# How the opening's shared query rows are loaded: 32 rows in place of 31, and ahead of the query tiles

## The chip, the cores and the metric

The kernel runs on one core of a Trainium2 chip. A core has a matrix engine (TensorE, PE in the profile), a vector engine (VectorE, DVE), a scalar engine for activations (ScalarE, ACT), a general engine (GpSimd, POOL) and SyncE (SP), which here does nothing but issue transfers. Each engine takes its instructions in order and waits for others by semaphores. Transfers between the chip's memory (HBM) and the on-chip memory (SBUF, 128 partitions) are made by 16 DMA engines that all issuing engines share. The metric is the device time of one execution in microseconds, taken as the median of several runs.

## The reference

The inputs are q, k and v of shape (8, 8, 576, 64): 8 batches, 8 heads, 576 rows, 64 columns. An attention without a score matrix is followed by a Fourier mixing block with a feed-forward layer:

```
q_s = softmax(q) over the 64 columns of a head
k_s = softmax(k) over the 576 rows
kv  = k_s^T v                      per batch and head, 64 x 64
x   = q_s kv                       laid out as (8, 576, 512)
u   = x + real(fft(fft(x, rows), columns))
out = u + relu(layernorm(u) @ w_ch1) @ w_ch2      w_ch1 512 x 2048, w_ch2 2048 x 512
```

All is float32.

## The kernel before

The eight batches are worked through one after another: while TensorE multiplies the feed-forward layers of one batch, the attention and the Fourier block of the next are prepared. The first batch has nothing to hide behind, so it has an opening of its own. Every step of the program carries a time as a number; the steps are sorted by it and each engine executes its share in exactly that order (a schedule written by hand, the text `OPENING`). The numbers set the order only: nothing waits for a clock, everything waits for data.

The opening loads, all issued by SyncE in the order that the list `order` in `loads_first` gives, unless it is said otherwise:

- four key tiles `ks` (L305), 128 partitions of 576 numbers, 288 KB each
- two query tiles `own` (L314), 128 partitions of two rows of 512 numbers, 512 KB each; tiles A and B of the script come from the first, C and D from the second
- the shared rows `tail`: the Fourier block folds row s with row 576 - s, and what does not fit in the tiles of 128 is collected from two batches in one tile, 4 groups of 32 partitions. The first partition of each group is a special row (row 0 or row 288 of a batch), the other 31 are consecutive rows. The function `shared` loads the 31 rows of each group (L295, four transfers), `shared_firsts` the four first rows (L298, issued by ScalarE as its first instruction)
- the values `v` in two column halves; each half is a transfer of 512 rows (L309) and one of the last 64 rows (L310)
- three tables of cosines and sines (L342 to L346), then eleven pieces of the feed-forward weights, called words (L369, 512 KB each), and behind these the keys and values of batch 1 (L676, L688) and more words (L371)

The weights come as 64-bit words and are converted on the chip (`convert`: ScalarE L396 and L397, VectorE L390 and L393, GpSimd L398); later words take the place of converted ones, so their loads are issued as conversions finish.

The computation of the opening, in the order of TensorE: transposes of the keys' exponentials (L561, L569), transposes of query tiles A and B (L984), products of keys and values for heads 0 to 3 (L585), transposes of C (L984), products for heads 4 to 7 (L585), transposes of D, then query times kv for the tiles (L839) and the transposes of the shared tile t. VectorE takes the maxima of the key tiles (L553) and of A, B, C, D and t in this order (L967); GpSimd subtracts them for A, B and C, VectorE for D and t (L972); ScalarE takes the exponentials (L976). VectorE scales the product (L588) once all of L585 is done. The matrix engine is also given a few products without a use (`warm`, L269).

For later batches the shared rows are loaded by `t_rows`: four transfers of 32 rows issued by SyncE (L337), and the four first rows later, on SyncE too (L338).

Of the kernel before, what the change touches and what calls it, by code (L numbers as in the profile page):

```python
# [46 lines left out]
P = 128  # L47
B, H, S, DH = 8, 8, 576, 64
# [10 lines left out]
Q = 32  # L59
# [79 lines left out]
class _Block:  # L139
# [134 lines left out]
    def loads_first(self, fetch):  # L274

        nc, b = self.nc, 0
        at = 2 * NF * D

        def place(n):
            nonlocal at  # L280
            at += n
            return self.big[:, at - n:at]

        own = [place(2 * D).rearrange("p (c n) -> p c n", n=D) for _ in range(2)]
        tail = place(D)
        at = 3 * NF * D - 5 * P - NC * D - NR * S
        ks, v = [place(S) for _ in range(NR)], place(NC * D).rearrange("p (c n) -> p c n", n=D)
        self.at_start = ks, v, own, tail
        load = nc.sync.dma_start

        def shared():
            flat = self.q[b:b + 2].rearrange("b s n -> (b s) n")
            for i in range(4):
                a = i * S // 2 + P
                load(tail[i * Q + 1:(i + 1) * Q], flat[a + 1:a + Q])  # L295

        def shared_firsts():
            nc.scalar.dma_start(tail[0:P:Q], self.q[b:b + 2].rearrange("b s n -> (b s) n")[::S // 2])  # L298

        def table():  # L300
            t = self.small.tile([P, 1], F32, tag="root", name="root", bufs=1)
            nc.scalar.activation(t[:], self.eps[:], ACT.Exp)

        def keys(r):
            load(ks[r], self.kT[b, r * P:(r + 1) * P, :])  # L305

        def values(r):
            cols = slice(r * P, (r + 2) * P)
            load(v[:, 0:4, cols], self.v[b, 0:512, cols].rearrange("(c p) n -> p c n", p=P))  # L309
            load(v[64:, 4, cols], self.v[b, 512:, cols])  # L310

        def queries(i):
            fours = self.q[b].rearrange("(a p) n -> p a n", a=2)
            load(own[i], fours[(1, S // 2 - P)[i]:(1, S // 2 - P)[i] + P])  # L314

        each = lambda f: [lambda r=r: f(r) for r in range(NR)]
        order = [shared_firsts, lambda: nc.gpsimd.memset(v[0:64, 4, :], 0.0), table, *each(keys), lambda: queries(0), lambda: queries(1),
                 shared, lambda: values(0), lambda: values(2), self.tables, *(lambda i=i: fetch(i) for i in range(11))]
        later = [step for _, step in self.keys_to(1) + [(0, self.prepare)] + self.values_to(1, 0)]
        return [(i / 100, step) for i, step in enumerate(order)] + [(18 + i / 100, step) for i, step in enumerate(later)]  # L320

# [147 lines left out]
    def load(self, n):  # L469

        if n >= len(self.plan):
            return
        k = (n + 3) % 4
        w = self.big[:, k * NP * HD:(k + 1) * NP * HD]
        self.nc.sync.dma_start(w[:, :self.plan[n].shape[1]], self.plan[n])
        self.stream[n] = w.rearrange("p (a n) -> p a n", n=HD)
# [1516 lines left out]
```

## Time and profile before

| | us |
|---|---|
| median of 3 runs | 1017.97 |
| lowest and highest run | 1017.58, 1018.14 |
| the profiled execution | 1019.2 |
| its span, first to last instruction | 1017.4 |
| busy: PE, DVE, ACT, POOL | 994.0, 718.5, 495.3, 442.1 |

All times of the trace are microseconds from the start of the span. "SPq" is SyncE's queue, whose only instructions are the issues of transfers; the duration of one is the time that the issue held the queue, not that of the transfer. PEld is the loading of weights into TensorE. The granted clock is the share of full speed at which TensorE was allowed to run. The idle time in square brackets at the end of a row is how long the engine stood before it, and what ended that. Where an engine waits for several things, the profile names the one that came last by its reckoning.

### The profile page before, as it was taken

The numbers are of one execution on the slowest core, as the hardware profiler recorded it, in microseconds if no ns is written. First come the engines' busy times: TensorE is split into PE (matmuls) and PEld (weight loads), VectorE is DVE, ScalarE is ACT, GpSimd is POOL, SyncE is SP. The second block draws the span as 40 slices with busy tenths as digits, with TensorE's granted clock in tenths as the row PEclk, the third lists the DMA queues.
The fourth block names the chain that finished last, engine by engine and source line by source line (L and its number), as shares of the span: only waits on it lengthen the run. The fifth ranks groups of instructions, "written<-read, shape, count | busy, mean of one in ns | idle before, by whom it ended". The sixth has DMA issues, their size and how long they took to land.

```text
span 1017.4 us, 19783 instructions
## 1 busy us (share of the span) xinstructions
PE 994.0 (98%) x7546; PEld 853.8 (84%) x7546; DVE 718.5 (71%) x1355; ACT 495.3 (49%) x1285; POOL 442.1 (43%) x445
## 2 busy tenths in 40 slices
PE   5899999999999899999999999999999999999998
PEld 4764454788888799889988998899888998998897
DVE  4888898657675687678756886678656935685563
ACT  4576633682368327751776257724782242151200
POOL 3354430258445547465656556564646360040000
PEclk7999999999999999999999999999999999999999
DMA  7977499686999757776769577947654755675573
GB/s 229 264 259 257 158 244 328 228 234 217 322 328 241 243 198 263 222 223 225 270 213 253 195 258 246 259 175 262 230 187 167 263 194 198 225 268 183 181 253 131
DMA packets 123495, 236.36 MB, mean 232 GB/s; under 512 B 24124, under 2 KB 88380, under 8 KB 112776
## 3 DMA queue, kind: packets, MB, share of 16 engines
q1 hardware_dynamic: 123024, 234.56, 70.8%
q8 instruction: 60, 0.98, 0.4%
q14 instruction: 35, 0.29, 0.1%
q10 hardware_dynamic: 296, 0.27, 0.1%
q0 software_dynamic: 80, 0.26, 0.1%
HBM read 199.93 MB, written 39.06 MB: 235 GB/s over the span
## 4 chain that ended last, share of the span: by engine, by line
PE 85%; DVE 7%; DMA 4%; issue 1%; SPq 1%; POOL 1%; ACT 1%; DVEq 0%; POOLq 0%
PE bb L1543 15%; PE ba L1543 10%; PE bc L1543 10%; PE bb L1670 10%; PE ba L1670 7%; PE bc L1670 7%; PE bb L1640 5%; PE bc L1478 2%; PE two L839 2%; DMA big<-w1s 2%; PE one L754 2%; PE two L1206 1%; PE two L1263 1%; PE bb L1759 1%; PE ba L1478 1%; PE ba L1759 1%
## 5 line engine op out<-in xcount | busy, mean ns | idle before, releaser
L1543 PE MATMUL bb<-unT,big 128*128 128x256 f32 x768 | 183.2, 380 | 0.2 <-DVE u L1513 0.2
L1543 PEld LDWEIGHTS bb<-unT,big 128*128 128x128 f32 x768 | 144.8, 190 | 21.0 <-DVE u L1513 1.0
L1555 ACT ACTIVATE big<-big 128x512 f32<-128x512 f32 x96 | 59.8, 629 | 147.7 <-DVE big L1554 141.1
L1543 PE MATMUL ba<-unT,big 128*128 128x256 f32 x512 | 124.1, 382 | 2.8 <-DMA big<-w1s 2.7
L1543 PE MATMUL bc<-unT,big 128*128 128x256 f32 x512 | 121.5, 380 | 0.1
L816 ACT ACTIVATE qT<-q 32x128 f32<-32x128 f32 x384 | 117.9, 307 | 5.9 <-DVE q L806 0.7
L1543 PEld LDWEIGHTS ba<-unT,big 128*128 128x128 f32 x512 | 95.4, 190 | 17.0 <-DMA big<-w1s 3.2
L1543 PEld LDWEIGHTS bc<-unT,big 128*128 128x128 f32 x512 | 96.9, 190 | 13.7 <-DVE big L1554 0.5
L1513 DVE TENSOR_TENSOR u<-bb,s 128x512 f32<-128x512 f32 x66 | 45.2, 685 | 88.3 <-PE bb L1543 70.6
L1670 PE MATMUL bb<-big 128*128 128x128 f32 x848 | 103.8, 276 | 0.2 <-DVE u L1677 0.2
L1670 PEld LDWEIGHTS bb<-big 128*128 128x128 f32 x848 | 98.9, 192 | 1.0 <-DVE u L1677 1.0
L1389 POOL COPY unT<-unT 32x256 f32<-32x256 f32 x98 | 42.0, 428 | 91.4 <-DVE unT L1381 87.2
L1620 POOL TENSOR_TENSOR x<-x,big 128x512 f32<-128x512 f32 x45 | 61.0, 1368 | 46.0 <-DVE big L1677 19.7
L1616 DVE TENSOR_TENSOR big<-big 128x512 f32<-128x512 f32 x98 | 79.9, 843 | 0.0
L1670 PE MATMUL ba<-big 128*128 128x128 f32 x640 | 79.0, 276 | 0.0
L1670 PEld LDWEIGHTS ba<-big 128*128 128x128 f32 x640 | 75.0, 192 | 0.8
L1389 ACT COPY unT<-unT 32x256 f32<-32x256 f32 x126 | 50.7, 402 | 32.1 <-DVE unT L1381 30.3
L803 POOL TENSOR_TENSOR q<-q,qm 128x512 f32<-128x512 f32 x24 | 25.8, 1073 | 91.1 <-DVE qm L798 55.7
L404 POOL TENSOR_TENSOR big<-big 128x512 f32<-128x512 f32 x24 | 30.4, 1268 | 68.8 <-ACT big L1555 68.8
L1640 PE MATMUL bb<-big 128*128 128x256 f32 x256 | 58.3, 379 | 0.0
L1554 DVE TENSOR_TENSOR big<-bc,u 128x512 f32<-128x512 f32 x64 | 44.0, 688 | 16.5 <-PE bc L1543 15.7
L1640 PEld LDWEIGHTS bb<-big 128*128 128x128 f32 x256 | 48.0, 190 | 6.1
(335 smaller groups left out, 1914.5 us busy)
## 6 DMA issues: line engine op xcount, KB each, us to landing
big<-w2d SPq DMA_DIRECT2D x67, 1024.0 KB
big<-w1s SPq DMA_DIRECT2D x64, 896.0 KB
big<-w2s SPq DMA_DIRECT2D x16, 1024.0 KB
big<-in_w_dram SPq DMA_DIRECT2D x21, 512.0 KB
w2d<-big SPq DMA_DIRECT2D x42, 256.0 KB
kb<-in_kT_dram SPq DMA_DIRECT2D x28, 320.0 KB
q<-in_q_dram SPq DMA_DIRECT2D x28, 256.0 KB
vt<-in_v_dram SPq DMA_DIRECT2D x84, 80.0 KB
```

The source lines that it names most:

```text
L404: e1.tensor_tensor(out=to(4), in0=at(2), in1=at(3), op=ALU.add)
L816: nc.scalar.activation(to[t, i * Q:i * Q + Q], one, ACT.Exp)
L1389: copy(to, of)
L1478: nc.tensor.matmul(po[:], lhsT=h[:, f, i * P:(i + 1) * P], rhs=self.w2sb[:, f, :], start=(f == 0), stop=(f == NF - 1))
L1513: plus = lambda t: V.tensor_tensor(out=temp(t), in0=box["bb"][:], in1=box["s1"][:], op=ALU.add)
L1543: nc.tensor.matmul(bank()[:, i, :], lhsT=w[:, WA_AT[m], k * P:(k + 1) * P], rhs=self.unT[g][:, B_AT[m], k, :], start=first and i == 0 and ...
L1554: steps = [(0, lambda: V.tensor_tensor(out=hp(i), in0=bank()[:], in1=u()[:], op=ALU.add)), (0.8, lambda: nc.scalar.activation(hp(i), hp(i) ...
L1555: (0.8, lambda: nc.scalar.activation(hp(i), hp(i), ACT.Relu))]
L1616: e.tensor_tensor(out=to(o), in0=to(x), in1=to(y), op=op)
L1620: E.tensor_tensor(out=x, in0=x, in1=tile(m), op=ALU.add)
L1640: nc.tensor.matmul(box[name][:, i, :], lhsT=h[p][:, A_AT[m], i * P:(i + 1) * P], rhs=self.stream[n][:, p, :], start=p == 0 and (m != 1 or ...
L1670: nc.tensor.matmul(box[place[n]][:, i, :], lhsT=own(m)(A_AT[n])[:, f, :], rhs=w[:, r // 2, r % 2 * P:r % 2 * P + P], start=first and f == ...
```

## The change

Each of the four transfers of shared rows takes 32 rows in place of 31, beginning with partition 0 of its group, so that it writes the group's first partition as well, with a row that does not belong there. The step moves from behind the two query tiles to ahead of them. The step that loads the four special rows, now issued by SyncE in place of ScalarE, moves from the start of the list to where the shared rows stood, behind the query tiles, and writes the right rows over the wrong ones. The transfers of keys, queries, values, tables and words keep their sizes and their order among themselves.

```
         def shared():
...
-                load(tail[i * Q + 1:(i + 1) * Q], flat[a + 1:a + Q])
+                load(tail[i * Q:(i + 1) * Q], flat[a:a + Q])

         def shared_firsts():
-            nc.scalar.dma_start(tail[0:P:Q], self.q[b:b + 2].rearrange("b s n -> (b s) n")[::S // 2])
+            load(tail[0:P:Q], self.q[b:b + 2].rearrange("b s n -> (b s) n")[::S // 2])
...
-        order = [shared_firsts, lambda: nc.gpsimd.memset(v[0:64, 4, :], 0.0), table, *each(keys), lambda: queries(0), lambda: queries(1),
-                 shared, lambda: values(0), lambda: values(2), self.tables, *(lambda i=i: fetch(i) for i in range(11))]
+        order = [lambda: nc.gpsimd.memset(v[0:64, 4, :], 0.0), table, *each(keys), shared, lambda: queries(0), lambda: queries(1),
+                 shared_firsts, lambda: values(0), lambda: values(2), self.tables, *(lambda i=i: fetch(i) for i in range(11))]
```

## The prediction

> **What bounds the kernel now.** I read the page first for the whole (the chain that ended last is 85% TensorE), then the same chain cut to the first 60 us, because only the opening's loads are touched. Columns: start us, duration us, what the chain stood on.
>
> ```profile
> PE 85%; DVE 7%; DMA 4%; issue 1%; SPq 1%; POOL 1%; ACT 1%; DVEq 0%; POOLq 0%
> ```
> ```profile
> 4.83 3.75 SPq L295
> ...
> 8.63 12.45 DMA big<-in_v_dram
> ...
> 21.13 2.40 PE two L585 x40
> 23.53 1.05 PE tr L984 x4
> 24.58 1.98 PE two L585 x40
> 26.55 0.58 PE tr L984 x4
> 27.14 0.64 PE two L839 x32
> ...
> 58.56 3.75 DMA big<-in_w_dram
> ```
>
> From 4.83 to 21.13 us the chain is SyncE issuing the fourth shared transfer (L295) and then the first value load (L309 and L310), which needs 12.45 us. Only then do the products of keys and values (L585) start. The time line of SyncE's queue and the stretches say why (start, duration; then per stretch: length, busy us of PE, PEld, DVE, ACT, POOL, granted clock, DMA share, GB/s):
>
> ```profile
> 3.61 4.97 SPq L295 DMA_DIRECT2D big<-in_q_dram  x4
> 8.63 2.41 SPq L309 DMA_DIRECT2D big<-in_v_dram  x1
> 11.08 2.46 SPq L310 DMA_DIRECT2D big<-in_v_dram  x1
> 13.59 0.58 SPq L309 DMA_DIRECT2D big<-in_v_dram  x1
> 14.21 2.32 SPq L310 DMA_DIRECT2D big<-in_v_dram  x1
> 20.06 10.19 SPq L369 DMA_DIRECT2D big<-in_w_dram  x8
> ```
> ```profile
> 10.00:11.50 1.50, 0.13 (x2) 0.00 (x0) 1.41 (x3) 0.96 (x2) 1.50 (x2) 1.00 0.07 26
> 16.00:20.00 4.00, 0.00 (x0) 0.00 (x0) 0.00 (x0) 0.00 (x0) 0.00 (x0) 0.50 0.84 269
> 55.00:60.00 5.00, 5.00 (x25) 4.41 (x24) 4.86 (x8) 5.00 (x10) 2.71 (x3) 1.00 0.16 56
> ```
> ```profile
> DMA packets 19, 0.04 MB, mean 26 GB/s; under 512 B 0, under 2 KB 0, under 8 KB 19
> ```
>
> Between 10.0 and 11.5 us the only traffic is 19 packets (the last line is for that stretch), one per 79 ns, and the mean share of the 16 DMA engines is 0.07, which is one engine of sixteen. So the four shared transfers of 31 rows, 124 packets of one 2 KB row, run on a single engine: 124 x 79 ns = 9.8 us. SyncE's issues stall behind them (2.41, 2.46 and 2.32 us where the same kind costs 0.58), every later transfer has a part queued on that engine, and between 16 and 20 us all compute engines stand still.
>
> By the Trainium skill, "DMA: Bandwidth & Descriptors", section "Why a DMA increments its semaphore by 16 and not by 1", a transfer issued from SyncE is spread over the largest number of engines up to 16 that divides its outer dimensions: 31 rows get one engine, 32 rows sixteen. The trace agrees on the 31 rows (share 0.07).
>
> **The change, part by part.**
>
> (a) *32 rows instead of 31.* Do 32 rows spread? The kernel has such transfers later (L337, four of 32 rows, and L338, which waits for their landing):
>
> ```profile
> 549.86 2.14 SPq L337 DMA_DIRECT2D q<-in_q_dram  x4
> 557.98 0.58 SPq L338 DMA_DIRECT2D q<-in_q_dram  x1
> ```
>
> 128 packets of 79 ns on one engine are 10.1 us; these had landed 8.1 us after the first issue, in a full queue. So they ran on more than one. I take full spreading. The pace comes from VectorE's waits, where the fourth key tile lands at 7.29 and the first query tile at 8.70:
>
> ```profile
> 3.60 1.53 DVE L553 TENSOR_REDUCE km<-big 128x1 f32<-128x576 f32 x2 [2.45 <-DMA big<-in_kT_dram]
> 7.29 0.75 DVE L553 TENSOR_REDUCE km<-big 128x1 f32<-128x576 f32 x1 [0.60 <-DMA big<-in_kT_dram]
> 8.70 1.28 DVE L967 TENSOR_REDUCE qm<-big 128x8 f32<-128x512 f32 x2 [0.65 <-DMA big<-in_q_dram]
> 11.51 1.28 DVE L967 TENSOR_REDUCE qm<-big 128x8 f32<-128x512 f32 x2
> 20.27 0.69 DVE L967 TENSOR_REDUCE qm<-big 128x8 f32<-128x512 f32 x1 [7.48 <-DMA ft<-in_ft_dram]
> 20.87 1.28 DVE L972 TENSOR_TENSOR big<-big,qm 128x512 f32<-128x512 f32 x2
> ```
>
> 512 KB in 1.41 us. The shared rows are 256 KB, so 0.70 us in place of 9.8 us.
>
> (b) *Ahead of the queries.* Keys keep their place. Shared rows land at 7.29 + 0.70 = 8.0, queries at 8.70 + 0.70 = 9.4 and 10.8. That delays the first query tile's chain (maximum, subtract, exponential, transpose) by 0.70 us. Before, it was hidden behind the wait for values; now it counts.
>
> (c) *First rows behind them on SyncE.* The issue leaves ScalarE's queue, where nothing waited for it: nothing gained. On SyncE it writes into rows that the four transfers write, so it has to wait until these land. The same pattern later does wait:
>
> ```profile
> SPq L338 <- DMA q<-in_q_dram: 11.0, 3, 5.4
> ```
>
> Behind the waiting instruction stand the values, tables and words. Wait until 8.0 to 8.2, issue 0.6 (L338 above 0.58), so values are issued from about 8.8, against 8.63 before: no loss. Their data queue behind the queries anyway: 10.8 + 1.41 (512 KB) + 0.18 (64 KB) = 12.4 for the first pair, 14.0 for the second. Bounds: 12.4 by the stream, 13.1 if the first one takes from its issue at 8.8 as long as the first key tile (issued at 0.74, seen at 3.60: 2.86 us for 288 KB) plus 0.8 for the larger size and 0.6 for a late issue. I take 12.4 to 13.1.
>
> (d) *What is late next.* TensorE takes its work in the written order: transposes of A and B, then the products.
>
> ```profile
> 11.58 1.71 PE L984 MATMUL tr<-ident,big 128*128 128x128 f32 x8 [1.45 <-ACT big L976]
> 26.27 0.28 PE L585 MATMUL two<-big 128*64 128x64 f32 x4
> 25.41 0.43 PE L585 MATMUL two<-big 128*64 128x64 f32 x4
> ```
> ```profile
> 9.18:12.59 3.41, 1.79 (x11) 1.19 (x11) 3.31 (x7) 2.17 (x5) 2.36 (x3) 0.96 0.28 88
> 12.59:16.00 3.41, 0.70 (x4) 0.30 (x2) 0.19 (x1) 1.40 (x3) 1.38 (x5) 0.50 0.65 197
> 19.42:22.83 3.41, 1.70 (x32) 1.71 (x34) 1.89 (x3) 1.23 (x2) 0.00 (x0) 0.50 0.90 296
> 22.83:26.24 3.41, 3.41 (x54) 2.96 (x52) 1.06 (x3) 0.58 (x1) 0.00 (x0) 0.54 0.95 295
> 26.24:29.66 3.42, 3.42 (x144) 2.93 (x142) 2.59 (x8) 1.28 (x3) 0.53 (x2) 1.00 1.02 310
> ```
>
> A's transposes move from 11.58 to 12.28. The granted clock falls to 0.50 near 12.6, and as 9.2 to 12.6 gets no busier I keep that. Four transposes cost 0.58 at full and 1.05 at half clock (chain above): A ends about 13.3, B 14.35. Values are there by 13.1, so the products start at 14.35, not 21.13: 6.8 us earlier.
>
> The clock then decides the rest. Before, a stretch of 3.41 us that was half busy (1.70) was followed by 0.50, one wholly busy (3.41) by 1.00. Now 12.6 to 16.0 is wholly busy, so I take full clock from 16.0. Four products cost 0.28 against 0.43, a factor 0.65. First forty: 14.35 + 1.65 at half, the rest 0.75 x 0.65 = 0.5, end 16.5. C's transposes 0.6, 17.1. Second forty 2.40 x 0.65 = 1.56, 18.65. D's transposes 0.58: the product at 27.14 starts at about 19.25. Shift: 27.14 - 19.25 = **7.9 us**.
>
> The window of about 3.41 us after which sustained work lifts the clock is what the Trainium skill states ("TensorE: Matmul & The Clock Gate", "Part 1: The HAM clock gate"); the trace agrees in that both clock changes lie on borders of such stretches.
>
> VectorE and ScalarE are no bound; the rows of before:
>
> ```profile
> 21.58 1.23 ACT L976 ACTIVATE big<-big 128x512 f32<-128x512 f32 x2 [7.09 <-DVE big L972]
> 22.85 0.69 DVE L945 TENSOR_REDUCE qrec<-big 128x8 f32<-128x512 f32 x1 [0.70 <-ACT big L976]
> 33.23 1.71 PE L1216 MATMUL two<-ft,eo 128*128 128x144 f32 x12
> ```
>
> Maxima of C and D end at 12.8 + 0.7 = 13.5, the shared maximum (0.69) at 14.2, the two subtractions at 15.45, ScalarE's two exponentials (1.23) by 16.1, the sums (0.69 and two small steps) by 17.3, and the normalizing is wanted only after 18.65. The shared rows have long landed, so the wait until 20.27 goes.
>
> (e) *After the opening.* All order is by dependence, so the shift should carry on if the DMA stream keeps up: the three tables, 1043 KB by their shapes, end at 14.0 + 2.9 = 17 (first used at 33.23 before, so at 25.3 now), eleven words of 1.41 us at 32.5. The next load on the chain, the word at 58.56, is issued when a conversion frees its place, and in 55 to 60 us the DMA engines are at share 0.16, so there is room. The rest of the chain, 85% of it TensorE, holds no work tied to a time of its own.
>
> **Sum.** The profiled execution has a span of 1017.4 and took 1019.2 us; 1019.2 - 7.9 = 1011.3. It stands 1.2 above the median of the runs, 1017.97, so against that: 1017.97 - 7.9 = **1010.1 us**.
>
> **Rivals.**
>
> *The clock stays at half* until 19.4: first forty end 16.75, C 17.8, second forty 19.9, D 20.5; gain 6.65, time 1011.3. Until 26.2: D ends at 21.25 and the next 2.4 us of TensorE (L839 and transposes) take 1.3 more; gain 4.6, time 1013.4. For it: the clock kept 0.50 for 13.6 us before. Against: two of those four stretches were idle or nearly so.
>
> *The DMA stream does not follow*, since first word, next keys and values queue as before. Then the fetch at 58.56 is late instead. Before it SyncE issued this:
>
> ```profile
> 49.38 3.90 SPq L371 DMA_DIRECT2D big<-in_w_dram  x3
> ```
>
> That ends at 53.28, 5.3 us before 58.56. Were it not to move at all, the gain is 5.3: 1012.7 us. Against: the issues at 8.63 to 20.06 lose their stalls.
>
> *Slower: 32 rows still on one engine, ahead of the queries.* 128 packets of 79 ns from 7.29 end at 17.4; the first query tile lands at 8.70 + 10.1 = 18.8, B's transposes end at 14.35 + 9.4 = 23.8, the products start 2.6 us later than before: 1020.6. It decides from a shared transfer longer than about 7.5 us. Against: the 8.1 us above.
>
> *No change*: the values wait on something else than that engine, and 21.13 stays. Against: share 0.07 at 10 to 11.5.
>
> **How the numbers follow.** Forecast 0.62, its own range 1009.0 to 1011.0; clock late 0.19; stream behind 0.11; slower 0.04; no change 0.03; 0.01 for a gain over 9 us (no drop to half clock at 12.6). Forecast, late clock and part of the stream's case give 1008.6 to 1013.2. A change of 0.2% (2.0 us) is about what can be told from none. Faster: 0.62 + 0.19 + 0.11 + 0.01 = 0.93.
>
> **What would show it.** Shared transfers issued at about 0.4 us each without a stall near 4 us; a wait of SyncE before the first rows ending near 8; DMA above 250 GB/s from 10 to 12; VectorE's first query maximum near 9.4; L585 starting near 14.3; clock 1.00 from 16; L839 near 19.3; the word's fetch near 50.7. I am wrong if L585 starts after 16, or if the shift at 60 us is smaller than at 20.

## The result and the profile after

The changed kernel took 1008.68 us (median of 4 runs, 1007.74 to 1011.98), the kernel before 1017.78 us beside it. The ratio is 0.9925 with a 95% interval of 0.991 to 0.9941: 7.6 us faster, between 6.0 and 9.2. (Amounts in us that stand beside a ratio are worked out from it. The two medians alone lie 9.1 us apart.) Two later series of the same kernel gave 0.9922 (0.9909 to 0.9935) and 0.9933 (0.9919 to 0.9946). The forecast was 7.9 us.

The profiled execution took 1011.98 us with a span of 1010.2, so it lies at the upper end of its runs, as the profiled one of before did. Its span is 7.2 us shorter. SyncE's queue and the chain of the opening after the change (start, duration):

```profile
0.74 1.82 SPq L305 DMA_DIRECT2D big<-in_kT_dram  x4
2.60 1.82 SPq L295 DMA_DIRECT2D big<-in_q_dram  x4
4.47 0.94 SPq L314 DMA_DIRECT2D big<-in_q_dram  x2
8.76 0.69 SPq L298 DMA_DIRECT2D big<-in_q_dram  x1
9.50 0.39 SPq L309 DMA_DIRECT2D big<-in_v_dram  x1
...
13.26 9.75 SPq L369 DMA_DIRECT2D big<-in_w_dram  x7
```
```profile
4.47 5.39 DMA big<-in_q_dram
9.88 0.70 DVE qm L967
10.65 1.05 POOL big L972
11.73 0.64 ACT big L976
12.76 0.63 PE tr L984 x4
13.42 1.11 PE tr L984 x4
14.53 2.33 PE two L585 x40
16.87 0.59 PE tr L984 x4
17.45 1.31 PE two L585 x40
18.77 0.59 PE tr L984 x4
19.36 0.64 PE two L839 x32
```

The four shared issues hold the queue for 1.82 us together, where the last one alone held it for 3.75, and the values no longer stall it. The chain now runs from the first query tile through its maximum, subtraction, exponential and transposes into the products. The first product of a query tile (L839) starts at 19.36 in place of 27.14 us, 7.8 us earlier. The stretches that stood still or moved 26 GB/s before are at work now (columns as in the prediction):

```profile
10.00:12.00 2.00, 0.49 (x4) 0.25 (x3) 1.94 (x5) 0.27 (x1) 1.35 (x2) 1.00 0.76 248
16.00:20.00 4.00, 4.00 (x99) 3.40 (x96) 2.08 (x5) 1.92 (x4) 0.00 (x0) 0.90 1.04 376
```

Further on, the chain reaches the first transposes behind the conversions at 110.88 in place of 118.51 us, still 7.6 earlier. From some 345 us on, the two kernels run in step, 6.7 us apart. The difference arises near 331 us, behind a wait of TensorE for weights (w1s). These are the chain of before, the chain of after, and one stretch of after:

```profile
322.33 16.11 DMA big<-w1s
...
338.49 1.13 PE ba L1543 x4
339.62 1.73 PE bb L1543 x8
...
352.70 3.45 PE bb L1640 x16
```
```profile
313.99 16.11 DMA big<-w1s
...
331.58 3.10 PE bb L1543 x8
...
346.03 3.45 PE bb L1640 x16
```
```profile
330.00:334.00 4.00, 3.86 (x11) 3.10 (x12) 0.00 (x0) 0.59 (x1) 3.92 (x4) 0.60 0.66 200
```

The transfer takes the same 16.11 us, but in this execution the clock fell behind it, so that eight products took 3.10 us in place of 1.73. None of the other profiles below has a fall of the clock there. It belongs to that execution and not to the change.

TensorE itself stood idle in front of these products for 2.74 us before and 2.36 us after. In the twelve other profiles of this document the same wait is between 0 and 1.84 us (1.84 and 0.87 in the two repeats of the change, 0 in two of the variants). So a microsecond or two that the opening wins can be lost or doubled there; no run varied what sets this wait.

### The profile page after: what moved, and what is told of

It is laid out like the page before. It is cut to its first block, busy times and chain, and to the rows that moved or that the text cites. A ratio compares the mean times of both kernels' runs of the same rounds, so it can differ in the third digit from the quotient of the medians.

```text
span 1010.2 us, 19785 instructions
## 1 busy us (share of the span) xinstructions
PE 995.2 (99%) x7546; PEld 855.0 (85%) x7546; DVE 716.1 (71%) x1355; ACT 495.3 (49%) x1285; POOL 443.4 (44%) x445
## 4 chain that ended last, share of the span: by engine, by line
PE 84%; DVE 7%; DMA 3%; ACT 3%; issue 1%; POOL 1%; SPq 0%; DVEq 0%; POOLq 0%
PE bb L1543 15%; PE bb L1670 10%; PE ba L1543 10%; PE bc L1543 10%; PE ba L1670 7%; PE bc L1670 7%; PE bb L1640 5%; PE bc L1478 2%; PE bb L1759 2%; DMA big<-w1s 2%; ACT qT L816 2%; PE two L839 1%; PE two L1206 1%; PE two L1263 1%; PE one L754 1%; PE ba L1478 1%
## 5 line engine op out<-in xcount | busy, mean ns | idle before, releaser
L1543 PEld LDWEIGHTS bc<-unT,big 128*128 128x128 f32 x512 | 96.9, 190 | 13.7 <-DVE big L1554 0.5
L1389 ACT COPY unT<-unT 32x256 f32<-32x256 f32 x126 | 50.7, 402 | 31.3 <-DVE unT L1381 29.5
L1640 PE MATMUL bb<-big 128*128 128x256 f32 x256 | 58.3, 379 | 0.0
L1640 PEld LDWEIGHTS bb<-big 128*128 128x128 f32 x256 | 48.0, 190 | 6.1
```

Of the source, the lines that this page charges most:

```text
L1389: copy(to, of)
L1543: nc.tensor.matmul(bank()[:, i, :], lhsT=w[:, WA_AT[m], k * P:(k + 1) * P], rhs=self.unT[g][:, B_AT[m], k, :], start=first and i == 0 and ...
L1640: nc.tensor.matmul(box[name][:, i, :], lhsT=h[p][:, A_AT[m], i * P:(i + 1) * P], rhs=self.stream[n][:, p, :], start=p == 0 and (m != 1 or ...
```

## The experiments

**The changed kernel again**, beside the first variants, and once more beside the last ones.

> The changed kernel once more, beside the kernels it is to be compared with. If the gain is what the opening's trace shows (27.14 to 19.36 us at the first L839, 7.8 us), the time is 7 to 8.5 us under before, about 1010, and the 9.1 us of the first runs was partly the scatter of executions. If there is a gain outside the opening, it stays at 9 us or more.

> The changed kernel a third time, beside the last two variants. By its earlier runs 6.9 to 9.1 us under before; the first query maximum between 9.9 and 10.8, L585 between 14.5 and 15.6, as where the queries' bytes happen to land moves it.

It was 6.9 us under before in the one series and 6.3 us in the other by medians (1010.0 against 1016.94, 1009.66 against 1015.95). The gain is, within a microsecond, what the opening shows. The first query maximum came at 10.80 and 9.79 us, the products at 15.54 and 14.54, L839 at 20.83 and 20.24, both later than the 19.29 of the first profile. In both, the granted clock was at half for longer, which is the rival "until 19.4":

```profile
16.00:18.00 2.00, 2.00 (x39) 1.88 (x36) 0.79 (x3) 1.85 (x4) 0.13 (x1) 0.50 1.02 379
18.00:20.00 2.00, 2.00 (x40) 1.67 (x42) 0.95 (x3) 0.59 (x1) 0.00 (x0) 0.77 1.08 374
```

(the first of the two). Whether the clock comes back near 17 or near 19 us changes from execution to execution of one kernel.

**The rows without the move.**

```
-        order = [..., *each(keys), shared, lambda: queries(0), lambda: queries(1),
-                 shared_firsts, lambda: values(0), ...
+        order = [..., *each(keys), lambda: queries(0), lambda: queries(1),
+                 shared, shared_firsts, lambda: values(0), ...
```

> 32 rows as changed, but behind the query tiles as before, the first rows right behind them on SyncE. My theory (one DMA engine carried the 31 rows; the new order matters only through the wait before the first rows): the shared rows land after the queries, near 10.9, SyncE waits until then, values are issued near 11.9 and land near 15.6; L585 starts at 15 to 16 in place of 14.5, the half clock lasts longer, L839 at 20.5 to 21.7; time 1 to 2.5 us above the changed kernel, 5.5 to 7 us under before. Rival (the order is what helps, since the stream of one engine then runs under the queries): L585 stays near 21 and the gain is under 2 us. Rival (order without any effect): the same as the changed kernel within 0.5 us.

1010.89 us, ratio 0.9942 (0.9929 to 0.9955), 5.9 us under before. Its queue and its products:

```profile
11.21 0.69 SPq L298 DMA_DIRECT2D big<-in_q_dram  x1
11.95 0.39 SPq L309 DMA_DIRECT2D big<-in_v_dram  x1
```
```profile
15.46 1.12 PE L585 MATMUL two<-big,kb 128*64 128x64 f32 x16 [2.54 <-DMA big<-in_v_dram]
```

SyncE waits until 11.2 for the shared rows, and TensorE then waits 2.54 us for values, as my theory said. So the 32 rows carry most of the gain (the interval overlaps that of the change), and behind the queries the wait before the first rows is no longer covered.

**The move without the rows.**

```
-        order = [shared_firsts, ..., *each(keys), lambda: queries(0), lambda: queries(1),
-                 shared, lambda: values(0), ...
+        order = [shared_firsts, ..., *each(keys), shared, lambda: queries(0), lambda: queries(1),
+                 lambda: values(0), ...
```

> Only the move: 31 rows per transfer as before, ahead of the query tiles, the first rows still on ScalarE at the start. My theory: about 10 us of one engine now stand before the queries too; first query maximum at 18 to 19, L585 at 23 to 24.5, 1 to 3.5 us slower than before (1019 to 1021.5). Rival (getting the shared rows early is what helped): L585 earlier than 21.1 and faster than before.

1019.48 us, ratio 1.0025 (1.0016 to 1.0034): 2.5 us slower. The first query maximum:

```profile
18.67 1.28 DVE L967 TENSOR_REDUCE qm<-big 128x8 f32<-128x512 f32 x2 [11.11 <-DMA big<-in_q_dram]
```

With 31 rows the transfers hold up the queries as they held up the values before. The products started at 23.42. This is the rival "slower" of the prediction in the flesh: it had 18.8 and 23.8 us, and 2.6 us of loss. That the loss in time agrees to 0.1 us is partly chance: the clock came back at 24.66, before at 26.00, so that L839 started only 0.7 us later (27.78), and about 1 us more is the gap described below.

**31 rows, spread in another way.** The kernel before, each transfer cut in two, first rows on ScalarE:

```
-                load(tail[i * Q + 1:(i + 1) * Q], flat[a + 1:a + Q])
+                for m, n in ((1, Q // 2), (Q // 2, Q)):
+                    load(tail[i * Q + m:i * Q + n], flat[a + m:a + n])
```

> The kernel before with one edit: each transfer of 31 rows is cut into one of 15 and one of 16 rows; the order, and the first rows on ScalarE, as before, so that SyncE waits for nothing. My theory (the whole loss was that 31 rows run on one engine): no stall of SyncE after 3.6, first query maximum at 8.7 to 9.1, L585 at 13.4 to 14.0, L839 at 18.5 to 19.0; 0.5 to 0.9 us better than the changed kernel, 8 to 9 us under before. Rival (the move ahead of the queries is needed): L585 after 16 and less gain than the changed kernel.

1011.72 us, ratio 0.9944 (0.9931 to 0.9957): 5.7 us under before. That the same 31 rows without any reordering give most of the gain shows that their number as one transfer was the cause. But I had expected it to beat the change by 0.5 to 0.9 us, and it did not. Two things in its opening went otherwise than I thought. One is SyncE, which did not get through its eight short transfers without waits:

```profile
3.61 7.55 SPq L296 DMA_DIRECT2D big<-in_q_dram  x8
11.20 0.42 SPq L310 DMA_DIRECT2D big<-in_v_dram  x1
```
```profile
SPq L296 <- DMA big<-in_q_dram: 3.0, 2, 1.7
SPq L296 <- DMA big<-in_kT_dram: 1.1, 2, 0.6
```

They wait for keys and queries, tiles that they do not touch. The products started at 14.91, a microsecond late. The other is a gap in TensorE inside L839 (here L840, as the edit adds a line) that no releaser in the profile explains:

```profile
20.58 1.04 PE L840 MATMUL two<-pairs,big 64*64 64x65 f32 x54
23.59 1.34 PE L840 MATMUL two<-pairs,big 64*64 64x65 f32 x42 [1.97 <-issue]
```

The first two profiles of the changed kernel have the same gap, of 0.35 and 0.37 us, after 55 of the 96 products; its third profile and the kernel before have none.

**The gap.** The instruction queue of the profile moves one packet of 16 KB in this stretch, and where there is a gap, TensorE went on 1.4 to 1.6 us after the packet had ended (in the 15-and-16 kernel the packet ran from 21.11 to 22.00, and TensorE went on at 23.59). The 1.1 to 1.3 us in the first expectation below are too small. Two variants of the 15-and-16 kernel hold words back until VectorE has written a number into a word's place, behind the normalizing of the shared tile (the second one, the first keeps words 0 and 1 where they were):

```
-                 ..., self.tables, *(lambda i=i: fetch(i) for i in range(11))]
-        return [...]
+                 ..., self.tables]
+        held = [lambda: nc.vector.memset(self.w2sb[0:1, 0, 0:1], 0.0), *(lambda i=i: fetch(i) for i in range(11))]
+        return [(14.801 + i / 1000, step) for i, step in enumerate(held)] + [...]
```

> The kernel with 15 and 16 rows, whose L839 stood 1.97 us for no releaser at 21.62, with the words from the third on held back: a small write into the third word's place, by VectorE behind the normalizing of the shared tile, must come before they are loaded (near 20 us). Theory (the stall is the load of TensorE's next instructions, 16 KB on the instruction queue, landing late because the word loads fill the DMA engines; in the runs so far TensorE goes on 1.1 to 1.3 us after that packet ended): the instruction packet moves ahead of 20.5 and the stall is under 0.5 us; the steps after it come 1.5 to 3.5 us earlier. Rival (the load of instructions follows TensorE's own progress): packet at 21.4 and stall as before.

> The kernel with 15 and 16 rows and all eleven words held behind a small write of VectorE after the normalizing of the shared tile, so that the DMA engines run empty before it (with two words let through they never did). Theory (full DMA engines delay TensorE's 16 KB of instructions): the packet starts before 20 and the stall of 1.97 us inside L839 falls under 1 us. Rival (the packet follows TensorE's own progress): it starts 2.0 us after the first L839, as in both runs with 15 and 16 rows, and the stall stays.

With two words let through the DMA engines stayed full (387 and 383 GB/s from 19 to 21 us), the packet still started 1.8 us behind the first of these products, as without the hold, the gap was 1.97 us again, and the time 1011.39 us (0.9939, 0.9921 to 0.9958): it told nothing apart. With all words held (1010.24 us, 0.9941, 0.9926 to 0.9957) the engines ran empty, and the gap was gone (stretches, then the products, here L841):

```profile
19.00:20.00 1.00, 1.00 (x36) 0.78 (x35) 0.95 (x3) 0.44 (x1) 0.00 (x0) 1.00 0.09 31
20.00:21.00 1.00, 1.00 (x36) 0.80 (x32) 0.76 (x3) 0.42 (x2) 0.00 (x0) 1.00 0.00 0
```
```profile
20.62 1.63 PE L841 MATMUL two<-pairs,big 64*64 64x65 f32 x96
```

The packet started at 18.79 in place of 21.11, as the data ran out, with L841 starting at 19.41 and L840 at 19.36. So the rival, a packet that always comes behind the first of these products, does not hold. But full engines alone do not make the gap: in the third profile of the changed kernel, and in the kernel before, they were as busy just ahead of the packet (383 and 292 GB/s), and yet there was none. What goes with the gap in all fourteen profiles is when the packet starts: in the ten with the gap behind the first product of L839 (by 0.16 to 1.80 us), in the four without it ahead of it (by 0.39 to 1.60 us). That a full stream makes the packet late fits this and is not shown by itself; when TensorE asks for the packet the profile does not show. In the time the removed gap is not seen (0.9941 against 0.9944).

**The wait before the first rows.**

```
-                 shared_firsts, lambda: values(0), lambda: values(2), self.tables, ...
+                 lambda: values(0), lambda: values(2), shared_firsts, self.tables, ...
```

> The changed kernel with the first rows moved behind the values, so that SyncE does not wait between queries and values. My theory (values are there before TensorE wants them, since the transposes of A and B end last): values are issued from 5.4 in place of 9.5, and L585 still starts with the end of B's transposes, 14 to 15.7; time within 1.5 us of the changed kernel. Rival (the wait costs something): L585 more than 1 us earlier. Rival (values issued earlier take bandwidth from the queries): first query maximum later than 10.8, and slower.

1011.33 us, ratio 0.9934 (0.9914 to 0.9953), and values issued from 6.28 us did not start the products earlier (15.29). So no cost of SyncE's wait for the shared rows is seen, as the forecast had it. The first query maximum came at 10.70, inside what the changed kernel itself shows.

**The idle stretch and the clock.**

```
-WARM = (2, 4, 256), (7.26, 1, 64), (8.52, 1, 64), (18.63, 2, 256), (22.111, 10, 256)
+WARM = (2, 4, 256), (7.26, 1, 64), (8.52, 1, 64), (11.845, 4, 256), (18.63, 2, 256), (22.111, 10, 256)
```

> The changed kernel with eight more products without a use (four calls, 256 columns) ahead of A's transposes, where TensorE stands idle between 10.5 and 12.7 us. Theory (the fall to half clock near 12.5 follows from the idle stretch before it, and costs about 0.35 of 2.3 plus 1 us): the clock stays at 1.00 through 16, L585's first forty take 1.4 in place of 2.3; 0.8 to 1.6 us faster to L839 than the changed kernel. Rival (the clock falls anyway): no change, or a loss where the added products end after A is ready.

This missed its aim. The added products write a tile that VectorE had to release first (L572), so they ran from 12.93 to 16.2 and not before 12.6:

```profile
12.93 3.46 PE L269 MATMUL tr<-pairs 128*128 128x256 f32 x8 [2.81 <-DVE big L572]
21.24 0.70 PE L839 MATMUL two<-pairs,big 64*64 64x65 f32 x32
```

L839 began at 21.24, 1.9 us later than in the first profile of the change, yet the time was 1010.45 (0.9934, 0.9915 to 0.9953), that of the changed kernel. It is one of the two variants in which TensorE does not wait for w1s near 330 us, and its L1640 started at 345.00, against 346.03 in the first profile of the change.

What this run leaves open, the profiles together show. In all fourteen, one change of the clock follows another after 3.41 us or a multiple of it, so I cut them into stretches of 3.41 us from there. Each fall in an opening, eleven in all, stands behind a stretch in which PE was busy for 1.9 us or less, and so does the one near 331 us. Behind a stretch with 1.94 us or more the clock never fell; between 1.5 and 1.9 us it fell in some and not in others. From half it came back behind stretches with 2.7 us or more only, and in two cases not even then (2.76 and 3.21). The limits are read off, with some overlap, and no run set them on purpose. Two stretches of the first profile of the change, then one of its third:

```profile
9.97:13.38 3.41, 1.14 (x8) 0.70 (x8) 3.31 (x7) 1.63 (x3) 2.04 (x2) 1.00 0.79 244
13.38:16.79 3.41, 3.38 (x45) 2.93 (x44) 2.38 (x4) 2.74 (x5) 1.71 (x5) 0.50 0.93 314
```
```profile
12.02:15.43 3.41, 2.76 (x24) 2.46 (x26) 3.38 (x6) 2.57 (x6) 2.28 (x6) 0.50 1.01 354
```

The first is followed by half clock, the second by full clock, the third by another stretch at half. The stretches lie otherwise against the program in each execution (the falls of the one kernel come at 13.38, 12.07 and 12.02), and with them the time at which the clock comes back, 16.8 or 18.9 us.

**Better orders.** First everything behind the queries, and the first rows behind the values; then, in addition, on VectorE the subtraction of D ahead of the shared maximum and L588 ahead of the shared sums; last, that one with all words held behind L588.

```
-                 *each(keys), shared, lambda: queries(0), lambda: queries(1),
-                 shared_firsts, lambda: values(0), lambda: values(2), self.tables, ...
+                 *each(keys), lambda: queries(0), lambda: queries(1), shared,
+                 lambda: values(0), lambda: values(2), shared_firsts, self.tables, ...
...
-... 13.00 t max, 13.10 D less, 13.20 t less, ... 14.75 t inverse, 14.76 k0 scale, 14.8 t normal, ...
+... 12.96 D less, 13.00 t max, 13.20 t less, ... 14.74 k0 scale, 14.75 t inverse, 14.8 t normal, ...
```

> 32 rows on 16 engines, but behind both query tiles, then the values, and the first rows behind the values, so that neither queries nor values stand behind a wait. Theory (pace is set by the first query tile, then by the values): first query maximum at 8.5 to 9.2, L585 at 13.2 to 14, L839 at 18 to 19; 0.5 to 1.5 us better than the changed kernel at L839. If the stall of TensorE inside L839 (0.35 us there, 1.97 in the kernel with 15 and 16 rows), which nothing in the profile releases, is a fixed point in the stream of transfers, it grows by what L839 gains, and the time is not better.

> The order with everything behind the queries (shared rows, values, first rows), and on VectorE the subtraction of D ahead of the shared maximum, and the scaling of the product (L588) ahead of the shared tile's sums, so that the late first rows hold up only the shared tile. L588 near 16.5 in place of 18.4, first L839 near 17, the shared tile's transposes near 18.5 in place of 19.5; 0.5 to 1.5 us better than the kernel it is made from, if the stall inside L839 does not grow by as much; 8 to 10 us under before.

> The reordered kernel with all eleven words held behind a small write of VectorE after the scaling of the product (L588), so that the DMA engines run empty about when TensorE's instructions are loaded. Theory (what still costs the opening time is the instruction packet behind the words): the gaps of 1.06 us and 0.64 us in which TensorE waits for no releaser go, and the steps near 30 us come 1 to 1.7 us earlier; words end later than in the reordered kernel but before the conversions want them; time 0.5 to 1.7 us under the reordered kernel, 9 to 10 us under before. Rival (the words are wanted early): the load on the chain near 52 us comes later and the gain is gone.

1009.18 us (0.9919, 0.99 to 0.9938), 1007.88 us (0.9925, 0.9911 to 0.9938) and 1008.57 us (0.9919, 0.9905 to 0.9933). The openings got shorter: the first L839 at 18.87, 16.70 and 17.63 us. The first of them, in SyncE's queue and VectorE's first query maximum:

```profile
5.81 0.53 SPq L309 DMA_DIRECT2D big<-in_v_dram  x1
6.82 0.58 SPq L310 DMA_DIRECT2D big<-in_v_dram  x1
8.10 0.39 SPq L309 DMA_DIRECT2D big<-in_v_dram  x1
10.18 0.48 SPq L310 DMA_DIRECT2D big<-in_v_dram  x1
11.38 0.62 SPq L298 DMA_DIRECT2D big<-in_q_dram  x1
```
```profile
8.11 1.28 DVE L967 TENSOR_REDUCE qm<-big 128x8 f32<-128x512 f32 x2 [0.45 <-DMA big<-in_q_dram]
```

But none is told from the change by its interval. In the second one TensorE stands 1.11 and 0.64 us, in the third 1.13 us, where the profile names no releaser. The 1.11 and 1.13 us are not the packet's: they stand ahead of the transposes of the shared tile, which the script puts behind its normalizing on VectorE (L956), and TensorE goes on 0.10 us after that has ended, in both. These are the lines of the second one:

```profile
17.72 0.69 DVE L956 TENSOR_TENSOR big<-big,qrec 128x512 f32<-128x512 f32 x1
18.51 0.63 PE L984 MATMUL tr<-ident,big 128*128 128x128 f32 x4 [1.11 <-issue]
```

So the price of the late first rows is a late shared tile. The 0.64 us are the gap of the packet, and they are gone in the third, where the packet started at 17.15, 0.48 us ahead of L840. The wait for w1s is 1.18, 1.45 and 1.09 us in the three.

## Why the prediction was right

**The cause.** The reading of 10 to 11.5 us, one engine of sixteen with a packet per 79 ns, carried the forecast, and the two halves of the edit bear it out: 31 rows ahead of the queries lose 2.5 us, 31 rows cut into 15 and 16 gain 5.7, 32 rows gain 5.9 without the move. That the move ahead of the queries is needed no run shows: the first of the better orders has the shared rows behind the queries, and its ratio is 0.9919.

**(a)** was right: four issues of 0.42 us, no stall, and the rows had landed by 8.76 us, 6.2 us after the first issue, while 128 packets of 79 ns on one engine would take 10.1 us.

**(b)** was too small. The move was to cost the first query tile 0.70 us (9.4); its maximum came at 9.88, 10.80 and 9.79 in the three profiles, and at 10.70 and 10.09 in the two variants with the same order up to there. In the four variants with 32 rows behind the queries it came at 8.48, 8.11, 8.34 and 9.60. Between the medians, 10.09 and 8.41, lie 1.7 us, more than twice the 0.70. The shared rows came 0.8 to 1.1 us behind the fourth key tile (forecast 0.70), the query tile then 1.1, 2.4 and 2.3 us behind them (forecast 1.41). Why the stream was slower is not shown.

**(c)** was right in kind. SyncE waited until 8.76, 8.38 and 7.50 (forecast 8.0 to 8.2), values were issued at 9.50, 9.12 and 8.24 (8.8), and TensorE never waited for them.

**(d)** was right in its result, but by errors that cancel, so that its exactness is partly luck. L585 started at 14.46 (forecast 14.35), L839 at 19.29 or 19.36 on the chain (19.25). The query tile was 0.5 us late, but the clock fell 0.8 us later than forecast (13.38), so that A's transposes ran at full clock. It came back 0.8 us later, too (16.79, forecast 16.0), but the second forty products then took 1.31 us in place of 1.56: the factor 0.65 was too high.

```profile
12.59:16.00 3.41, 3.21 (x36) 2.67 (x38) 3.14 (x6) 2.74 (x6) 1.82 (x6) 0.62 0.89 272
```

In the later two profiles the clock was at half from 12.1 to 18.9 and from 12.0 to 18.8 us, and L839 was 1.5 and 0.9 us later. Of this, 0.5 and 0.9 us arose between L585 and L839, where the clock decides; the rest of the 1.5 us is mostly a query tile that came 0.9 us later. The rival of the late clock, to which I gave 0.19, was so the case in two of three profiles, at a price of 0.5 to 0.9 us there, against the 1.25 us forecast for it.

**(e)** was right: the load that stood on the chain at 58.56 was issued at 50.84 (forecast 50.7; the chain of after goes by a load two further on, at 53.49), and the shift was 7.6 us at 110.88. The rival of the stream did not occur. What the step overlooked is the gap that goes with the instruction packet, 0.35 us in this profile, and the wait for w1s, which changes from profile to profile by more than 2 us.

**The sum.** 7.9 us was forecast; 7.6, 7.9 and 6.8 us follow from the three ratios. The median that was forecast, 1010.1 us, came out at 1008.68, below the range of 1009.0 to 1011.0 given to the forecast itself and just inside the wider one of 1008.6 to 1013.2; the two later series gave 1010.0 and 1009.66. So the agreement to 0.3 us in the first ratio is closer than the mechanism alone would earn.

## What to carry to other kernels

A stretch in which the mean share of the DMA engines stands near one sixteenth (here 0.07), with one packet behind the other, can be one transfer on one engine. Look then at its number of rows: here 31 rows gave it, and 32 rows, or 15 and 16, ended it, even at the price of writing a row twice. The same transfer set earlier without that cure does harm: with 31 rows ahead of the queries, their first maximum came at 18.67 in place of 8.70 us. When an opening is shortened, look again at what only the wait had covered: here the first query tile, the clock and the engines' own instructions. And look for a wait further on that moves by as much as you hope to win: here the one for w1s, 0 to 2.74 us.

## What the runs showed of the hardware that I had not expected

Loads of instructions stand in the profile among the transfers of the DMA engines. Where TensorE's packet of 16 KB started behind the first product of L839, TensorE stood 0.35 to 1.97 us in the middle of a group of products (ten profiles); where it started ahead of it, not at all (four, two of them with words held back, two with full engines).

Issues on SyncE waited for transfers that have nothing to do with theirs. In the first of the better orders the four value issues come at 5.81, 6.82, 8.10 and 10.18, the third of them when the first query tile lands (8.11). This fits a wait of each transfer for the one issued eight before it; no run varied that number.

The clock fell to half for 3.4, 6.8, 10.2 or 13.7 us in different executions, and in three variants (the first two of the better orders and the last) not at all in the opening. It fell behind stretches of 3.41 us in which PE was busy for up to 1.9 us, so the stretch need not be idle, and it came back only behind stretches busy for 2.7 us or more.
